# A DeltaNet and GELU-MLP kernel: the factors behind the GpSimd power, the bank of the second layer's last product, and the joins one block earlier

## The chip, the cores and the metric

The kernel runs on one core of one Trainium2 chip. The metric is device microseconds of one execution. Before the change the median of three runs is 658.57 us (658.12 to 659.23).

## The reference

Two parts, one after the other. The first is a DeltaNet layer over 4 x 8 sequences (batch x head) of 768 tokens with 48 channels each; the second is a two-layer MLP with exact GELU over the 3072 tokens, 384 -> 2048 -> 384. All is float32.

```python
k_n = k / (np.linalg.norm(k, axis=-1, keepdims=True) + 1e-06)
for t in range(S):                       # 768 steps, state (B, H, 48, 48)
    y[:, :, t] = einsum('bhd,bhde->bhe', q[:, :, t], state)
    v_old = einsum('bhde,bhd->bhe', state, k_n[:, :, t])
    state = state + beta_t * einsum('bhd,bhe->bhde', k_n[:, :, t], v_t - v_old)
x = y.transpose(0, 2, 1, 3).reshape(B * S, H * D)
h = x @ w_in
g = 0.5 * h * (1.0 + erf(h / sqrt(2)))
out = g @ w_out
```

## The kernel before, in words

**Tiling.** The 768 steps are cut into 12 chunks c of 64 tokens. A chunk has two units (a = 0, 1), each with two batches on the two halves of the 128 partitions and 8 heads. Within a chunk the recurrence becomes small matrix products: Gram products of the keys (`grams`), masked query-key products (`queries`, L459 puts the mask on them into P), a triangular system, and its solution. The system of two chunks, of four 32-row blocks a head, is handled at once: its 32 x 32 diagonal blocks are eliminated row by row (`eliminate`, L516 and L518, from chunk 4 on GpSimd), and the blocks below the diagonal are added by two *joins*, `join_both` (matmuls on L636): level 0 makes XM from G (results taken by VectorE on L648), level 1 makes Zf (L652). Around the elimination: `scales` (L486 and L491, needs the factors), `flip` (L496), `scaled_flip` (L501), then `back`: L527 turns Nu into XM, L531 into Zf, and L535 copies half of Zf on ScalarE.

**Factors.** The keys are not normalised; their factors gm are applied later. `norms` squares the keys on ScalarE, `prep` sums them on VectorE (L358) and takes the root as a power 0.5 on GpSimd (L360), and `finish` makes gm on VectorE (L307 to L311). `finish` waits for the power.

**The state.** For each chunk in turn: products with the state (psK, L710), subtraction (L721, L722, L727), `solve` (psU, L745; copied by ScalarE on L753 and L755), `use` and `update` (psY, L775 and L786), and `turns` (psX, L837), which transposes the outputs into xT for the MLP.

**The MLP.** From chunk 4 on it works on two chunks at once and uses a scheme with seven products for four blocks in both layers. The first layer runs in four blocks b; a block has eleven parts, in this order on TensorE (`part_of_layer`, matmuls on L977): P1 (X), P5 (Z), P6 (Y), P2 (X), R22 (Z), R11 (X), P7 (Y), P3 (V), R12 (V), P4 (Y), R21 (Y); the letters are PSUM tiles. P1, P5 and R22 are followed by copies on ScalarE; P6 by L1005 and L1036 on VectorE; P7 by L1013 (which reads Y and R22's copy, and before whose end P4 must not write Y) and a Gelu; R11 and R21 by Gelus; R12 by L1025. The second layer is seven products per chunk (matmuls on L911): 1 (X), 5 (Z), 2 (X), 6 (Y), 4 (X), 7 (Y), 3 (V). Its mixes of G are L1044, L1045 (mix 1), L1047 (mix 2) and L1049 (mix 3), its results are put together on L1079 to L1090; L1090 reads the last product, psV2.

**PSUM.** Eight banks: tag "dn" with two slots of two banks in rotation (psJ, psG, psK, psU, psY, psX of the DeltaNet part, and psV2), tag "mlp" with two slots, and one bank each for tags "z" and "sq"; psV of the first layer is in "sq".

**Order of the work.** Every step is put into a plan with a due time; one unit of time is one chunk. `emit` traces the steps by due time. VectorE's queue is exactly that order. The other engines' queues are set by a scheduler that starts from it; TensorE's MLP parts are chained, and `together` keeps steps of the DeltaNet part in one run on TensorE. Stage w (w = 4, 6, 8, 10) prepares chunks w and w+1 (elimination, joins, Gram products of w+2 and w+3, state) while the MLP of the chunks before runs. Due times of its steps are `begins`; n6, p6, n7, p7 are those of `norms` and `prep`; `turned_k` (L408) and `turned_q` (L413) transpose keys and queries on VectorE. Every engine takes its own queue in order, the DMA-issuing SP too.

Of the kernel before, what the change touches and what calls it, by code (L numbers as in the profile page):

```python
# [8 lines left out]
F32 = mybir.dt.float32  # L9
# [5 lines left out]
ALU = mybir.AluOpType  # L15
# [4 lines left out]
def kernel(  # L20
# [28 lines left out]
    nc = tc.nc  # L49
# [19 lines left out]
    small = [start.enter_context(tc.tile_pool(name="sq", bufs=2, space=bass.MemoryType.PSUM))]  # L69
    su = start.enter_context(tc.tile_pool(name="su", bufs=2))  # L70

    def dn(name):
        return ps.tile([128, 2, 512], F32, tag="dn", name=name)
# [225 lines left out]
    def heads(ap):  # L299
        return ap.rearrange("q (j r) d -> q r j d", r=2)  # L300
# [145 lines left out]
    def queries(us):  # L446
        c = us[0].c
        psP = products(us, 1)
        if c not in Ps:
            Ps[c] = (su if c == 1 else wk).tile([128, NA * H, C], F32, tag=f"P{c == 1}", name="P",  # L450
                                                bufs=1)
        for u in us:
            u.P = Ps[c][:, u.a * H:(u.a + 1) * H]
        dst = heads(Ps[c][:, us[0].a * H:(us[-1].a + 1) * H])
        if c < 2:
            nc.scalar.copy(dst, psP)
        else:
            both = mask.unsqueeze(1).to_broadcast([128, len(us) * H, C])
            nc.vector.tensor_tensor(dst, psP, heads(both), op=ALU.mult)  # L459

    def masked(u, engine=nc.gpsimd):
        engine.tensor_tensor(u.P, u.P, mask_h, op=ALU.mult)
# [163 lines left out]
    def join_both(g, level):  # L626

        xm, zf, off = XMs[g], Zf[g % 2], Gs[g]
        gm = gms[g].rearrange("q t h -> q (t h)")
        psJ = dn("psJ").rearrange("q b (k n) -> q b k n", n=2 * HB)  # L630
        for k in range(H):
            for cc in range(2):
                for p in range(2):
                    us = slice(2 * (cc * H + k), 2 * (cc * H + k) + 2)
                    rows = slice(p * C + level * HB, p * C + (level + 1) * HB)
                    nc.tensor.matmul(psJ[HALF[p ^ cc], p, k, :],  # L636
                                     lhsT=(xm if level else off)[rows, us, :],
                                     rhs=zf[rows, us, HB:C] if level else xm[rows, us, :],
                                     start=True, stop=True)
        for cc in range(2):  # L640
            for p in range(2):
                for e in range(2):
                    us = slice(2 * cc * H + e, 2 * (cc + 1) * H, 2)
                    at_ = (p ^ cc) * C + e * HB
                    src = psJ[at_:at_ + HB, p, :, e * HB:(e + 1) * HB]
                    if level == 0:
                        low_ = slice(p * C + HB, (p + 1) * C)
                        nc.vector.tensor_tensor(  # L648
                            xm[low_, us, :], src,
                            gm[low_, us].unsqueeze(2).to_broadcast([HB, H, HB]), op=ALU.mult)  # L650
                    else:
                        nc.vector.tensor_copy(zf[p * C:p * C + HB, us, HB:C], src)  # L652

    def gram_steps(c, part=(0,)):
        us = [tiles[c, a] for a in range(NA)]
# [193 lines left out]
    DH = DM // 2  # L849
# [50 lines left out]
    def of_g(c):  # L900
        g = Gp[c % 2 if c > 3 else 0]
        return [[g[:, a, k * FH:(k + 1) * FH] for k in range(2)] for a in range(NA)]

    W2 = {}
# [146 lines left out]
    def two(c, n):  # L1051
        A = of_g(c)
        if n == 1:
            W2["X"] = ps.tile([128, 2, DH], F32, tag="mlp", name="psX2")
            W2["o"] = [wk.tile([128, DM], F32, tag="o_sb", name="o_sb") for a in range(NA)]
            product(W2["X"][:, 0], A[0][0], B11, True)
        elif n == 5:
            W2["Z"] = small[0].tile([128, DH], F32, tag="z", name="psZ2")
            product(W2["Z"], W2["S"], T[1], True)
            W2["p1"] = more[0].tile([128, DH], F32, tag="p1", name="p1")  # L1060
            nc.scalar.copy(W2["p1"], W2["X"][:, 0])
        elif n == 6:
            W2["Y"] = ps.tile([128, 1, DH], F32, tag="mlp", name="psY2")
            product(W2["Y"][:, 0], A[0][0], T[2], True)
        elif n == 2:
            product(W2["X"][:, 0], A[0][1], B21, False)
        elif n == 7:
            product(W2["Y"][:, 0], A[1][0], T[3], False)
        elif n == 4:
            product(W2["X"][:, 1], A[1][1], T[4], True)  # L1070
        else:
            W2["V"] = dn("psV2")[:, 0, 0:DH]
            product(W2["V"], A[0][1], B22, True)

    def read2(c, n):
# [48 lines left out]
    def at(first, last, steps):  # L1124

        total, done, timed = sum(s[0] for s in steps), 0.0, []
        for w, *step in steps:
            timed.append((first + (last - first) * (done + 0.5 * w) / total, step))
            done += w
        return timed  # L1130
# [122 lines left out]
    def state_at(c, *times, first=(), second=()):  # L1253

        steps = state_steps(c, first, second)
        if len(times) > len(steps):
            steps = steps[:-1] + [(turn, tiles[c, a]) for a in range(NA)]
        return [(t, step) for t, step in zip(times, steps) if t is not None]

    plan = [at(c + 1 + 0.25 * (c == 1), c + 2 + 0.25 * (c == 0), ffn_steps(c)) for c in range(4)]  # L1260
# [31 lines left out]
    for c in range(3, NC):  # L1292
        t = c - (1.35 if c % 2 and c > 5 else 1.0)
        plan += [at(t, t + 0.01, [(1.0, load_v, c)])]
    for c in range(4, NC):
        us = [tiles[c, a] for a in range(NA)]
        even = c % 2 == 0
        for name, src, t in (("Kb", k, {4: 1.8, 5: 2.73, 6: 3.25, 7: 3.55}.get(c, c - (2.9 if even else 3.6))),
                             ("Qb", q, {4: 3.2, 5: 3.9}.get(c, c - (1.4 if even else 1.29)))):
            plan += [at(t, t + 0.01, [(1.0, load_blocks, c, name, src)])]  # L1300
        for name, t in (("Kn", {4: 2.1, 5: 2.74, 7: 4.24}.get(c, c - (2.1 if even else 2.84))),
                        ("Kp", {4: 3.6, 5: 4.3}.get(c, c - (0.6 if even else 0.85)))):
            plan += [at(t, t + 0.01, [(1.0, load_k, c, name)])]
        t = {4: 2.7262, 5: 2.955, 6: 3.5, 7: 4.31}.get(c, c - (2.7 if even else 2.98))
        plan += [at(t, t + 0.0005, [(1.0, turned_k, u) for u in us])]
        t = {4: 3.88, 5: 4.33}.get(c, c - (0.3 if even else 0.93))
        plan += [at(t, t + 0.01, [(1.0, turned_q, u) for u in us])]
    def gram(c):
        return [(grams, [tiles[c, a] for a in range(NA)])] if c < NC else []
# [1 line left out]
    def query(c):  # L1311
        return [(queries, [tiles[c, a] for a in range(NA)])]
# [18 lines left out]
    for c in (2, 3, *range(4, NC, 2)):  # L1331
        n = FH // blocks(c)
        for b in range(n):
            t = c + 1.06 + 0.2577 * b
            plan += [at(t, t + 0.001, [(1.0, add_p5)])]
        t = c + (1.42 if c < 4 else 1.93)
# [14 lines left out]
    for w in range(4, NC, 2):  # L1351
        more_to_come = w + 2 < NC
        if w == 4:
            begins = 0.21, 0.29, 0.36, 0.44, 0.52, 0.57, 0.63, 0.72, 0.82, 0.92
            n6, p6, n7, p7 = 0.2, 0.26, 0.43, 0.48
        else:
            begins = -0.21, -0.11, 0.0, 0.1, 0.21, 0.29, 0.38, 0.52, 0.67, 0.84
            n6, p6, n7, p7 = 0.15, 0.2, 0.38, 0.42
            t = -1.5 if w > 6 else -1.44
            plan += rows_of(w // 2, w, ((1, t, t + 0.001), (1, t + 0.02, t + 0.021), (1, t + 0.03, t + 0.031),  # L1360
                                        (31, t + 0.04, -0.6), (1, -0.29, -0.289), (1, -0.285, -0.284),
                                        (1, -0.283, -0.282)))
        begins = [w + t for t in begins]
        plan += [at(begins[0], begins[0] + 0.001, [(1.0, together, (join_both, w // 2, 0), *query(w))]),
                 at(begins[1], begins[1] + 0.001, [(1.0, together, (join_both, w // 2, 1), *gram(w + 2))]),
                 state_at(w, *begins[2:6], second=gram(w + 3)),
                 state_at(w + 1, *begins[6:], second=query(w + 1))]
        if more_to_come:
            plan += spread("gram", 2, begins[1] + 0.04) + spread("gram", 2, begins[1] + 0.06)
            plan += spread("gram", 4, begins[3] + 0.04)  # L1370
            plan += [at(w + n6, w + n6 + 0.001, [(1.0, norms, w + 2)]), at(w + p6, w + p6 + 0.001, [(1.0, prep, w + 2)]),
                     at(w + n7, w + n7 + 0.001, [(1.0, norms, w + 3)]), at(w + p7, w + p7 + 0.001, [(1.0, prep, w + 3)]),
                     at(w + p7 + 0.04, w + p7 + 0.041, [(1.0, finish, w + 2)])]
    with tc.manual_schedule(engines={mybir.EngineType.DVE}):
        emit(*plan)

# [29 lines left out]
```

## Time and profile before

| | us |
|---|---|
| median of the runs | 658.57 |
| the profiled execution | 658.88 |
| its span, first to last instruction | 656.3 |
| TensorE busy in the span | 616.1 |
| VectorE, ScalarE, GpSimd busy | 430.9, 247.7, 204.2 |
| stage 6: start of its MLP (280.2) to the start of the next (382.2) | 102.0 |
| stage 8: 382.2 to 484.4 | 102.2 |
| stage 10: 484.4 to 577.4 | 93.0 |
| MLP of chunks 10 and 11: 577.4 to 656.3 | 78.9 |

The stages hold the same MLP work; stages 6 and 8 have two runs of Gram products each that stage 10 lacks (64 matmuls in 1.09 us a run), and the last one has no DeltaNet work. A matmul's record begins when it starts and its modelled end can lie beyond the start of the next one, so the distance between the starts of two neighbouring parts is the time of the first: 0.87 us for a part of the first layer in stages 6 to 10, 2.6 for a product of the second, 1.09 for a run of 64 small matmuls.

### The profile page before, as it was taken

The page shows a single profiled execution, that of the slowest core. Times are in us where ns is not written, and L with a number is a line of the kernel's source. Part 1 is how long each engine was busy: PE and PEld are TensorE (multiplying, and loading weights), DVE is VectorE, ACT ScalarE, POOL GpSimd, SP SyncE. Part 2 cuts the span into 40 slices and gives each one's busy share as a digit, 9 for nine tenths or more (in the row PEclk, how much of TensorE's full clock was granted, in tenths as well). Part 3 has the DMA queues.
Part 4 walks back from the last instruction along what each step waited for, and adds up shares of the span by engine and source line. Part 5 has one row for each costly group of instructions (what it writes and reads, how often), then busy time and mean ns, then how long its engine had stood idle before and what let it go on. Part 6 is the DMA issues. An engine that isn't in the chain of part 4 may idle for free.

```text
span 656.3 us, 20825 instructions
## 1 busy us (share of the span) xinstructions
PE 616.1 (94%) x8998; PEld 550.1 (84%) x8998; DVE 430.9 (66%) x783; ACT 247.7 (38%) x552; POOL 204.2 (31%) x310
## 2 busy tenths in 40 slices
PE   5778999999999989899997999997999999999997
PEld 4666877766999988888797998797998789998997
DVE  6999989988757878445975554966542956332442
ACT  3576777424640453133632034442024422133300
POOL 4043002001588314882013884012686000000000
PEclk9568999999999989999998999999899999999999
DMA  9885673103443424231134321224120201010010
GB/s 134 173 264 156 130 188 109 25 2 63 70 70 54 86 36 69 54 65 21 17 55 70 73 53 23 25 41 72 38 49 1 25 3 25 3 25 1 0 25 24
DMA packets 158427, 39.69 MB, mean 60 GB/s; under 512 B 150016, under 2 KB 153216, under 8 KB 158336
## 3 DMA queue, kind: packets, MB, share of 16 engines
q1 hardware_dynamic: 155664, 37.34, 29.4%
q10 hardware_dynamic: 2672, 1.03, 0.8%
q8 instruction: 70, 1.15, 0.7%
q14 instruction: 21, 0.17, 0.1%
HBM read 33.62 MB, written 4.72 MB: 58 GB/s over the span
## 4 chain that ended last, share of the span: by engine, by line
PE 63%; DVE 20%; issue 8%; ACT 4%; DMA 2%; POOL 2%; SPq 1%; DVEq 0%; ACTq 0%; POOLq 0%
PE psX L911 10%; PE psY L977 9%; PE psX L977 7%; PE psY L911 6%; PE psZ L977 5%; PE psV L977 4%; PE psV L911 3%; DVE Nu L518 3%; DVE tmp L516 3%; PE psK L710 3%; PE psZ L911 3%; PE psO L878 2%; PE psH L860 2%; DVE XM L527 2%; PE psG L423 2%
## 5 line engine op out<-in xcount | busy, mean ns | idle before, releaser
L360 POOL TENSOR_TENSOR n<-n,half 128x16 f32<-128x16 f32 x10 | 30.0, 3003 | 218.8 <-DVE n L358 169.0
L518 POOL TENSOR_TENSOR Nu<-Nu,tmp 128x30 f32<-128x30 f32 (+14 forms) x120 | 65.1, 543 | 9.0
L516 POOL TENSOR_TENSOR tmp<-Nu 128x30 f32<-128x30 f32 (+14 forms) x120 | 61.9, 516 | 9.3
L977 PE MATMUL psX<-xT,w_in_sb 128*128 128x256 f32 (+1 forms) x288 | 62.8, 348 | 0.0
L911 PE MATMUL psX<-w_out_sb,G 128*128 128x192 f32 x320 | 60.3, 345 | 0.0
L911 PEld LDWEIGHTS psX<-w_out_sb,G 128*128 128x128 f32 x320 | 56.4, 202 | 0.8
L977 PEld LDWEIGHTS psX<-xT,w_in_sb 128*128 128x128 f32 x288 | 48.4, 193 | 5.1
L860 PE MATMUL psH<-xT,w_in_sb 128*128 128x256 f32 x192 | 44.3, 384 | 2.6 <-ACT G L960 2.0
L860 PEld LDWEIGHTS psH<-xT,w_in_sb 128*128 128x128 f32 x192 | 35.7, 190 | 9.8 <-ACT G L960 3.3
L878 PE MATMUL psO<-w_out_sb,G 128*128 128x384 f32 x128 | 43.9, 490 | 0.0
L1005 DVE TENSOR_TENSOR psY<-psY,pu 128x512 f32<-128x512 f32 x20 | 14.0, 698 | 43.3 <-PE psY L977 42.1
L977 PE MATMUL psY<-xT,w_in_sb 128*128 128x256 f32 (+1 forms) x192 | 41.6, 346 | 0.0
L960 ACT COPY xT<-psX 128x768 f32<-128x768 f32 x9 | 7.2, 800 | 89.8 <-PE psX L837 89.8
L960 ACT COPY pu<-psZ 128x512 f32<-128x512 f32 x40 | 23.5, 588 | 36.3 <-PE psZ L977 31.5
L878 PEld LDWEIGHTS psO<-w_out_sb,G 128*128 128x128 f32 x128 | 23.6, 190 | 14.0
L977 PEld LDWEIGHTS psY<-xT,w_in_sb 128*128 128x128 f32 x192 | 31.9, 191 | 3.3
L960 ACT ACTIVATE G<-G 128x512 f32<-128x512 f32 x40 | 25.2, 630 | 23.4 <-DVE G L1013 23.2
L1013 DVE TENSOR_TENSOR G<-psY,pu 128x512 f32<-128x512 f32 x20 | 13.8, 690 | 27.1 <-PE psY L977 26.9
L423 PE MATMUL psG<-Qt,Kt 48*64 48x64 f32 x768 | 18.0, 252 | 11.8 <-DVE o_sb L1090 7.7
L911 PE MATMUL psZ<-T,pu 128*128 128x192 f32 x160 | 28.3, 329 | 0.1
L911 PE MATMUL psY<-T,G 128*128 128x192 f32 x160 | 28.2, 329 | 0.0
L423 PEld LDWEIGHTS psG<-Qt,Kt 48*64 48x64 f32 x768 | 15.8, 163 | 14.6 <-DVE o_sb L1090 8.0
(197 smaller groups left out, 1384.2 us busy)
## 6 DMA issues: line engine op xcount, KB each, us to landing
Kp<-in_k_dram SPq DMA_DIRECT2D x76, 96.0 KB, 3.1
w_out_sb<-in_moe_w_in_dram SPq DMA_DIRECT2D x24, 256.0 KB, 4.2
w_raw<-in_moe_w_out_dram SPq DMA_DIRECT2D x16, 384.0 KB, 4.4
V<-in_v_dram SPq DMA_DIRECT2D x48, 96.0 KB, 3.1
out_dram<-o_sb SPq DMA_DIRECT2D x40, 96.0 KB, 2.2
Qp<-in_k_dram SPq DMA_DIRECT2D x64, 32.0 KB, 2.2
Qp<-in_q_dram SPq DMA_DIRECT2D x64, 32.0 KB, 2.1
Qp<-in_q_dram SPq DMA_DIRECT2D x16, 96.0 KB, 4.3
```

What stands on the lines that cost most here:

```text
L360: nc.gpsimd.tensor_tensor(flat, flat, half, op=ALU.pow)
L423: nc.tensor.matmul(psG[HALF[p], r, i * NP + j, :], lhsT=u.Kt[rows, p, j, :], rhs=(u.Qt if x else u.Kt)[rows, p, j, :], start=True, stop=True)
L516: rows_on.tensor_tensor(tmp, nu[:, j + 1:, j:j + 1].to_broadcast([128, n, j]), nu[:, j:j + 1, 0:j].to_broadcast([128, n, j]), op=ALU.mult)
L518: rows_on.tensor_tensor(nu[:, j + 1:, 0:j], nu[:, j + 1:, 0:j], tmp, op=ALU.add)
L710: nc.tensor.matmul(u.psK[to, x, r, j, :], lhsT=(u.Qt if x else u.Kt)[rows, p, j, :], rhs=St[rows, u.a, p ^ r, j, :], start=True, stop=True)
L860: nc.tensor.matmul(psH, lhsT=w_in_sb[:, f // 2, m, f % 2 * 128:(f % 2 + 1) * 128], rhs=xTs[c][:, m, :], start=(m == 0), stop=(m == NM - 1))
L878: nc.tensor.matmul(u.psO, lhsT=G[:, u.a, f, :], rhs=w_out_sb[:, f, :], start=(f == 0), stop=(f == NF - 1))
L911: nc.tensor.matmul(ps_, lhsT=lhs[:, f, :], rhs=rhs[:, f, :], start=first and f == 0, stop=f == FH - 1, skip_group_check=not first)
L960: i = fn(*args, **kw)
L977: nc.tensor.matmul(ps_[:, i], lhsT=lhs[:, f // 2, f % 2 * 128:(f % 2 + 1) * 128], rhs=rhs, start=first and i == 0, stop=True, skip_group_c ...
L1005: nc.vector.tensor_tensor(L1["Y1"], L1["Y1"], L1["pu"][:, 0], op=ALU.add)
L1013: nc.vector.tensor_tensor(half(1, 1), shaped(L1["Y1"]), shaped(L1["pu"][:, 0]), op=ALU.add)
```

## The change

Four things are edited.

1. psV2, the last product of the second layer, leaves the "dn" tag for the "sq" bank, which the first layer's psV uses.
2. The masking of the queries (L459) becomes a step of its own from chunk 4 on (`cover`), and the taking of a join's results (L648 or L652) becomes two steps (`take`), one per chunk of the pair. At level 0 the mask's step stands between the two halves.
3. In stages 6 to 10 the due times of both joins, of `back`, and of `against_state` of the first chunk move earlier, those of the elimination's start a little. L413 of even chunks moves earlier with them.
4. `prep` of the second chunk moves earlier and `finish` later, and L408 of chunk 7 and L413 of chunk 5 move later.

No instruction is added or removed on any engine. In VectorE's queue of stages 6 to 10 (L numbers of before): L413 twice, L1005, L1036, L527, L531, L1013, half of L648, L1025, L459, the other half of L648; later L1025 of the last block behind L721 and L727. In the second layer: L358 ahead of L1082, L1090 ahead of L307, and L1047 twice ahead of L459 and L496. On TensorE the first join and the query products stand between P7 and P3 of the third block (before: behind P1 of the fourth), the second join and the Gram products behind P6 of the fourth block (before: behind R22), and psK ahead of P3 (before: ahead of R21). On ScalarE L535 stands ahead of R22's copy of the third block (before: behind that block's P7 Gelu), and the squares of the second chunk ahead of L722. In stage 4 the second half of L648 follows L459, and L721 and L727 stand ahead of L408 and L413.

```diff
             both = mask.unsqueeze(1).to_broadcast([128, len(us) * H, C])
-            nc.vector.tensor_tensor(dst, psP, heads(both), op=ALU.mult)
+            masks[c] = lambda: nc.vector.tensor_tensor(dst, psP, heads(both), op=ALU.mult)
+            if c < 4:
+                masks[c]()
+
+    masks = {}
+
+    def cover(c):
+        masks[c]()
...
-        for cc in range(2):
+        def taken(cc):
             for p in range(2):
...
+        todo.append(taken)
+
+    todo = []
+
+    def take(cc):
+        todo[-1](cc)
...
-            W2["V"] = dn("psV2")[:, 0, 0:DH]
+            W2["V"] = small[0].tile([128, DH], F32, tag="sq", name="psV2")
             product(W2["V"], A[0][1], B22, True)
...
-        t = {4: 2.7262, 5: 2.955, 6: 3.5, 7: 4.31}.get(c, c - (2.7 if even else 2.98))
+        t = {4: 2.7262, 5: 2.955, 6: 3.5, 7: 4.38}.get(c, c - (2.7 if even else 2.98))
         plan += [at(t, t + 0.0005, [(1.0, turned_k, u) for u in us])]
-        t = {4: 3.88, 5: 4.33}.get(c, c - (0.3 if even else 0.93))
+        t = {4: 3.88, 5: 4.4}.get(c, c - (0.47 if even else 0.93))
         plan += [at(t, t + 0.01, [(1.0, turned_q, u) for u in us])]
...
         if w == 4:
             begins = 0.21, 0.29, 0.36, 0.44, 0.52, 0.57, 0.63, 0.72, 0.82, 0.92
-            n6, p6, n7, p7 = 0.2, 0.26, 0.43, 0.48
+            takes = 0.212, 0.214, 0.292, 0.294
+            n6, p6, n7, p7, f7 = 0.2, 0.26, 0.4, 0.44, 0.55
         else:
-            begins = -0.21, -0.11, 0.0, 0.1, 0.21, 0.29, 0.38, 0.52, 0.67, 0.84
-            n6, p6, n7, p7 = 0.15, 0.2, 0.38, 0.42
-            t = -1.5 if w > 6 else -1.44
+            begins = -0.33, -0.163, -0.06, 0.08, 0.21, 0.29, 0.38, 0.52, 0.67, 0.84
+            takes = -0.328, -0.255, -0.16, -0.158
+            n6, p6, n7, p7, f7 = 0.15, 0.2, 0.37, 0.41, 0.53
+            t = -1.46 if w > 6 else -1.44
             plan += rows_of(w // 2, w, ((1, t, t + 0.001), (1, t + 0.02, t + 0.021), (1, t + 0.03, t + 0.031),
-                                        (31, t + 0.04, -0.6), (1, -0.29, -0.289), (1, -0.285, -0.284),
-                                        (1, -0.283, -0.282)))
+                                        (31, t + 0.04, -0.6), (1, -0.42, -0.419), (1, -0.415, -0.414),
+                                        (1, -0.413, -0.412)))
         begins = [w + t for t in begins]
...
                  state_at(w + 1, *begins[6:], second=query(w + 1))]
+        plan += [at(w + t, w + t + 0.001, [(1.0, take, i % 2)]) for i, t in enumerate(takes)]
+        plan += [at(t, t + 0.001, [(1.0, cover, c)])
+                 for t, c in ((begins[0] + (0.004 if w == 4 else 0.07), w), (begins[7] + 0.03, w + 1))]
...
-                     at(w + p7 + 0.04, w + p7 + 0.041, [(1.0, finish, w + 2)])]
+                     at(w + f7, w + f7 + 0.001, [(1.0, finish, w + 2)])]
```

## The prediction

> **What bounds the kernel now.** I read the page's chain first, then TensorE's waits, then the timeline where the waits sit. All line numbers are those of the kernel before.
>
> ```profile
> PE 63%; DVE 20%; issue 8%; ACT 4%; DMA 2%; POOL 2%; SPq 1%; DVEq 0%; ACTq 0%; POOLq 0%
> ```
>
> Most of the chain is TensorE work, and from 280 us on nearly all of it. So a change pays there only if it removes TensorE idle time or half-clock time; both have to be found by place. The waits of TensorE (us in total, times, longest) name two that the change touches:
>
> ```profile
> PE psG L423 <- DVE o_sb L1090: 7.7, 2, 3.9
> ...
> PE psY L977 <- ACT G L960: 3.3, 3, 1.1
> ```
>
> The first falls in the second layer of stages 6 and 8 (a stage prepares chunks w and w+1; w = 4, 6, 8, 10). This is stage 6 (start, us, ..., [idle before <- releaser]):
>
> ```profile
> 352.08 1.15 PE L745 MATMUL psU<-V,Zf 64*64 64x48 f32 x64
> 357.10 1.98 PE L423 MATMUL psG<-Qt,Kt 48*64 48x64 f32 x64 [3.88 <-DVE o_sb L1090]
> 359.01 4.88 PE L911 MATMUL psX<-w_out_sb,G 128*128 128x192 f32 x16
> 363.73 2.76 PE L911 MATMUL psZ<-T,pu 128*128 128x192 f32 x16
> ...
> 354.80 0.18 DVE L307 TENSOR_SCALAR n<-n 128x32 f32<-128x32 f32 x1 [3.02 <-POOL n L360]
> ...
> 356.70 0.34 DVE L1090 TENSOR_TENSOR o_sb<-psV,o_sb 128x192 f32<-128x192 f32 x1
> ...
> 351.86 2.90 POOL L360 TENSOR_TENSOR n<-n,half 128x16 f32<-128x16 f32 x1 [12.56 <-DVE n L358]
> ```
>
> The query product psG needs the PSUM slot of the second layer's psV2, whose reader L1090 stands in VectorE's queue behind `finish` (L307 to L311), which waits 3.0 us for GpSimd's power (L360, 2.90 us). Meanwhile psX takes 4.88 us where its neighbour psZ, with as many matmuls, takes 2.76: the clock fell. The windows view shows when (stretch, its length, busy us of PE, PEld, DVE, ACT, POOL, then the granted clock):
>
> ```profile
> 233.44:236.85 3.41, 1.51 (x103) 1.39 (x95) 2.65 (x4) 0.49 (x1) 0.00 (x0) 1.00 0.15 21
> 236.85:240.27 3.42, 3.36 (x30) 3.26 (x30) 3.33 (x7) 1.35 (x3) 0.00 (x0) 0.50 0.29 35
> 264.15:267.57 3.42, 2.05 (x27) 1.84 (x18) 1.23 (x1) 1.28 (x5) 3.11 (x7) 1.00 0.29 55
> 352.90:356.32 3.42, 0.33 (x24) 0.20 (x16) 1.42 (x4) 1.89 (x6) 3.07 (x3) 1.00 0.26 44
> 356.32:359.73 3.41, 2.63 (x66) 2.51 (x67) 1.42 (x4) 0.00 (x0) 1.68 (x2) 0.50 0.27 61
> ```
>
> A stretch with TensorE busy 0.33 of 3.42 us is followed by half clock; so is one busy 1.51 of 3.41. One busy 2.05 of 3.42 is not.
>
> **Part 1: the bank, and `finish` moved behind L1090.** psV2 no longer rotates through the two-slot "dn" tag, so psG takes the slot of psK, whose readers (L721, L722) are done by 348 us. In the changed queue L358 stands ahead of L1082, and L1090 ahead of L307. Stage 10 has no `finish` and shows the undisturbed spacing: psU at 555.18, psZ at 559.91, 4.73 us. Stage 6 takes 352.08 to 363.73 = 11.65, stage 8 454.11 to 465.95 = 11.84. Gain 6.92 + 7.11 = **14.0 us** (per stage 3.9 idle, 0.9 of psG and 2.0 of psX at half clock). The new bank adds a wait of psV2 on L1025 (325 us, wanted at 349) and of the next layer's psV on L1090 (383.9, wanted at 388.2): nothing.
>
> What is late next: psY (L775) needs the mask L459, now its own step behind both L1047. In stage 6, on the old clock, psX would start at 354.3. The second L1047 ends some 3.6 us later, as in stage 10 (557.20; 560.11 + 0.69), at 357.9. L459 (1.23) ends at 359.1 and psY is due at 354.3 + 2.7 + 2.7 = 359.7. It fits by 0.6 us, if L307 to L311 (2.0 us), whose power now starts at about 349.4, end before 355.9; I cost it at nothing, and at 1 us per us that the power is late. The squares, moved up in ScalarE's queue, need the next chunk's keys: the four issues (2.7 us) start when the last squares end (335.7) and land 3.1 us later, 341.5, against 343.0. That cover is 1.5 us.
>
> **Part 2: the join moved into the third block.** Stage 6 before:
>
> ```profile
> 307.31 2.08 DVE L527 STREAM_TRANSPOSE XM<-Nu 128x1024 f32<-128x1024 f32 x1
> 309.27 1.95 DVE L531 STREAM_TRANSPOSE Zf<-Nu 128x1024 f32<-128x1024 f32 x1
> ...
> 309.62 1.16 PE L636 MATMUL psJ<-XM,G 32*64 32x64 f32 x64
> ...
> 311.25 2.10 ACT L535 COPY Zf<-Zf 32x1024 f32<-32x1024 f32 x2 [4.41 <-DVE Zf L531]
> ...
> 314.02 1.13 PE L977 MATMUL psY<-TX,Sw 128*128 128x256 f32 x4 [1.09 <-ACT G L960]
> ```
>
> The join costs about 1.3 us of idle here: 0.1 before L636, 1.1 at psY (its bank's Gelu stands behind L535 in ScalarE), 0.1 before the second join. Afterwards the first join and the query come after P7 of block 2, five products (4.3 us) earlier. In the changed queue of ScalarE, L535 stands *ahead* of R22's copy and R11's Gelu of that block, and VectorE does L531 ahead of L1013, which needs that copy. From the end of L527 (time 0): L531 1.95, L535 2.10, copy 0.6, L1013 0.7, hand-overs 0.1: L1013 ends at 5.4. TensorE joins at 0.2, then join and query 1.09 each, P3 0.97, R12 0.87: P4, which writes the bank that L1013 reads, is due at 4.25. **Idle 1.2 us.** Then half of L648 1.73, L1025 0.68, L459 1.23, the other half 1.73: XM is whole at 10.8, and the second join can start at 10.9. TensorE does P4, R21, P1, P5, P6 from 5.45 (4 x 0.87 + 0.97) and is due at 9.9. **Idle 1.0.** Behind that nothing is late: L652 (3.45) ends before psK is due.
>
> The first join itself waits for L527. Stage 6: L1036 ends at 303.5, GpSimd's rows at 298.5, L527 at 305.55; the slot is at 305.2 (P7 starts at 304.35): idle 0.6. Sum 2.8 against 1.3: **+1.4 us**.
>
> Stages 8 and 10: GpSimd now decides. Its elimination runs 38.6 us from L501 (362.36 to 400.96). In the changed stage 6, L496 follows L459 on a clock 1.4 us late: L501 at 359.1 + 1.9 + 0.1 + 1.4 = 362.5, hardly moved, while TensorE is 6.92 - 1.4 = 5.5 us ahead. The rows end at 401, L527 at 403, the join is at 403.2; its slot is at 406.38 + 0.87 - 5.5 = 401.7. Idle 1.5 + 1.2 + 1.0 = 3.7 against 1.3: **+2.4**. Stage 10 likewise (L501 4.5 us earlier than 464.39, rows end 498.5, join 500.8, slot 499.3): 3.7 + 0.15 against 1.9 (the page adds 0.6 before P4 there): **+1.9**. Stage 4: the second half of L648 now follows L459, so the second join waits 1.0 us, of which 0.3 is taken back where psK waits for L652 anyway: **+0.7**; the half-clock stretch after 236.85 may shift with it, worth up to 1.7 us less.
>
> **Other edits.** L413 earlier: Qt's data are long there (its loads end near 248 us for stage 6) and VectorE idles 3.7 us before L1005. On SP the key loads go ahead of the 16 query loads (8.7 us) and values stand among key blocks; the latest comer, the value rows for L385, lands near 354, and L385 stands before L491 and L501, which starts at 362: hidden by 4 us. On GpSimd two value products (0.83 us) move by up to two rows in stage 4. Instruction counts are the same on every engine. Nothing.
>
> **Sum.** -14.0 + 1.4 + 2.4 + 1.9 + 0.7 = -7.6 us. The profiled execution took 658.88 (span 656.3 and 2.6 around it), so 651.3; the median of the runs is 658.57, 0.3 lower: **651.0**.
>
> **A rule weighed.** The rows above show half clock after a TensorE idle of 1.96 us. The Trainium skill (TensorE: Matmul & The Clock Gate, "Why this matters for your kernels") warns only of idle gaps over about 3 us, because it wants one whole idle window. By it my 1.5 us waits never cost clock and the sum stays 651.0; by the rows they could, and a second rival has that price.
>
> **Rivals.**
> (a) The join's waits do not appear, as intended: then only the 14.0 is left, 644.5, and with the old 1.3 + 1.3 + 1.9 gone as well 640. For it: ScalarE and VectorE idle much in these blocks. Against: the order in their queues. 0.12.
> (b) One or two clock drops, or the mask late after a late power. A drop costs 2.9 us as at 356 (0.9 + 2.0). Stage 8's first join leaves TensorE busy 1.9 of 3.4 us if the wait falls in one stretch, between the 1.51 that dropped and the 2.05 that did not. 653.9 to 656.8. 0.22.
> (c) Slower: the clock drops at the joins of all three stages for two stretches each, 3 x 3.4 = 10.2, 661. It decides from a busy share under some 0.5 in each stage; stage 6, with 0.6 and 1.2 idle four us apart, speaks against. 0.08.
> (d) The drops take back the gain almost exactly, within 0.2%: 0.05.
>
> **Numbers.** Main case 0.53, at 648 to 654. A measurement tells 0.2% (1.3 us) from no change. Range 646.5 to 656.5: all of the main case, half of (a), nearly all of (b), about 0.8. Faster 0.53 + 0.12 + 0.22 = 0.87, same 0.05, slower 0.08.
>
> **What would show it.** Right: no wait of psG on L1090; full clock after 350 and 453 us; L1090 ahead of L307. Right for the joins: P4's psY waiting on L1013 by 1.2 us in three stages, L1013 waiting on ScalarE's copy behind L535; the second join waiting on L648; the first join in stages 8 and 10 waiting on L527, and L527 on GpSimd's L518. Wrong: psY (L775) waiting on L459, half clock beside a join, or no wait at P4.

## The result and the profile after

The changed kernel takes 648.82 us (median of 4 runs, 647.99 to 649.38) against 658.35 for the kernel before (4 runs, 658.05 to 659.23): ratio 0.985, 95% interval 0.9835 to 0.9869. That is 9.5 us less; 7.6 less, 651.0, was predicted. The profiled execution took 647.99, its span 646.3.

Kernels made from the changed one have its line numbers: L527, L531, L535 are now L534, L538, L542; L496 and L501 are L503 and L508; L518 is L525; L648 and L652 are L655 and L659; L1013, L1025, L1036 are L1027, L1039, L1050; L1047 is L1061; L1090 is L1104; L775 is L789; the matmul lines L636, L710, L745, L911 and L977 are L643, L724, L759, L925 and L991, and ScalarE's L960 is L974.

The second layer of stage 6 first (the timeline of the changed kernel; columns as before):

```profile
353.60 1.15 PE L759 MATMUL psU<-V,Zf 64*64 64x48 f32 x64
353.70 0.36 DVE L1104 TENSOR_TENSOR o_sb<-psV,o_sb 128x192 f32<-128x192 f32 x1 [1.32 <-PE psV L925]
353.98 0.17 DVE L307 TENSOR_SCALAR n<-n 128x32 f32<-128x32 f32 x1
354.56 1.13 PE L423 MATMUL psG<-Qt,Kt 48*64 48x64 f32 x64
355.62 2.87 PE L925 MATMUL psX<-w_out_sb,G 128*128 128x192 f32 x16
358.32 2.76 PE L925 MATMUL psZ<-T,pu 128*128 128x192 f32 x16
```

psU to psZ is 4.72 us (11.65 before). L1104 stands ahead of L307, psG starts when psU's matmuls are through, and psX takes 2.87 instead of 4.88: there is no half-clock stretch here any more. What TensorE now waits for from 280 us on (its waits; us in total, times, longest):

```profile
PE psY L991 <- DVE G L1027: 3.4, 3, 1.1
PE psJ L643 <- DVE XM L655: 1.6, 3, 0.5
PE psJ L643 <- DVE XM L534: 1.4, 3, 0.6
```

All three belong to the moved joins. The timeline of stage 6's third block shows the first two:

```profile
303.76 2.10 DVE L534 STREAM_TRANSPOSE XM<-Nu 128x1024 f32<-128x1024 f32 x1
305.92 1.16 PE L643 MATMUL psJ<-XM,G 32*64 32x64 f32 x64 [0.22 <-DVE XM L534]
307.75 2.10 ACT L542 COPY Zf<-Zf 32x1024 f32<-32x1024 f32 x2 [5.22 <-DVE Zf L538]
309.88 0.59 ACT L974 COPY pu<-psZ 128x512 f32<-128x512 f32 x1
310.49 0.69 DVE L1027 TENSOR_TENSOR G<-psY,pu 128x512 f32<-128x512 f32 x1 [2.78 <-ACT pu L974]
...
311.24 1.13 PE L991 MATMUL psY<-TX,w_in_sb 128*128 128x256 f32 x4 [1.15 <-DVE G L1027]
...
316.62 1.14 PE L643 MATMUL psJ<-Zf,XM 32*64 32x64 f32 x58 [0.53 <-DVE XM L655]
```

Read it backwards from P4 at 311.24: it waits for L1027, that for R22's copy at 309.88, and the copy for L542 ahead of it in ScalarE's queue, although R22's product was long done: its matmuls ended at 304.0, and ScalarE had idled 5.22 us until L538. In stage 8 the first join waits longer, and its L534 is now released by GpSimd:

```profile
400.46 2.08 DVE L534 STREAM_TRANSPOSE XM<-Nu 128x1024 f32<-128x1024 f32 x1 [0.32 <-POOL Nu L525]
...
402.60 1.16 PE L643 MATMUL psJ<-XM,G 32*64 32x64 f32 x64 [0.61 <-DVE XM L534]
```

On the page GpSimd's share of the chain grew from 2% to 11% accordingly:

```profile
PE 59%; DVE 21%; POOL 11%; issue 4%; DMA 2%; ACT 2%; SPq 0%; DVEq 0%; POOLq 0%
```

The stage lengths (start of a stage's MLP to the start of the next, from the profiled executions) tell the kernels apart more sharply than the medians do. The start of stage 6 itself lay between 278.3 and 282.2 us over 14 profiles, without any order that follows the edits, so what lies before it is left out. "rest" is stage 11 to the end of the span; "issue" is a TensorE wait in stage 8 for nothing that the profile shows, which some profiles have and others of the same kernel have not.

| kernel | stage 6 | stage 8 | stage 10 | rest | issue in stage 8 |
|---|---|---|---|---|---|
| before | 102.0 | 102.2 | 93.0 | 78.8 | |
| changed | 96.3 | 96.7 | 93.7 | 79.1 | |
| changed, second profile (after_again) | 96.3 | 96.9 | 93.7 | 79.0 | |
| bank | 95.1 | 95.1 | 93.0 | 78.8 | |
| finish | 95.1 | 95.3 | 93.0 | 78.8 | |
| bank_finish | 95.1 | 95.4 | 93.0 | 78.9 | |
| joins | 102.0 | 104.9 | 93.6 | 78.8 | 1.0 |
| prep_early | 96.7 | 96.7 | 93.1 | 78.9 | |
| after_copy_late | 94.0 | 94.6 | 91.5 | 79.0 | |
| copy_late_again | 94.0 | 95.8 | 91.5 | 78.8 | 1.0 |
| after_whole | 95.4 | 97.8 | 92.8 | 78.8 | 1.5 |
| after_flip | 97.9 | 98.9 | 93.3 | 79.0 | 0.6 |
| bank_copy_late | 94.6 | 95.4 | 92.8 | 78.8 | 1.3 |
| mask_first | 94.0 | 95.2 | 91.0 | 78.8 | 0.8 |

### The profile page after: what moved, and what is told of

Its sections match the earlier page's. It is cut to its first block, busy times and chain, and to the rows that moved or that the text cites. A ratio compares the mean times of both kernels' runs of the same rounds, so it can differ in the third digit from the quotient of the medians.

```text
span 646.3 us, 20824 instructions
## 1 busy us (share of the span) xinstructions
PE 614.1 (95%) x8998; PEld 547.5 (85%) x8998; DVE 428.8 (66%) x783; ACT 248.5 (38%) x552; POOL 203.3 (31%) x310
## 3 DMA queue, kind: packets, MB, share of 16 engines
HBM read 33.62 MB, written 4.72 MB: 59 GB/s over the span
## 4 chain that ended last, share of the span: by engine, by line
PE 59%; DVE 21%; POOL 11%; issue 4%; DMA 2%; ACT 2%; SPq 0%; DVEq 0%; POOLq 0%
PE psX L925 10%; PE psY L925 7%; PE psY L991 6%; POOL Nu L525 5%; PE psX L991 5%; POOL tmp L523 5%; PE psV L991 4%; PE psK L724 3%; PE psZ L991 3%; PE psV L925 3%; DVE Nu L525 3%; DVE tmp L523 3%; PE psZ L925 3%; PE psO L892 3%; PE psG L423 2%
## 5 line engine op out<-in xcount | busy, mean ns | idle before, releaser
L360 POOL TENSOR_TENSOR n<-n,half 128x16 f32<-128x16 f32 x10 | 30.0, 3002 | 209.6 <-DVE n L358 159.8
L525 POOL TENSOR_TENSOR Nu<-Nu,tmp 128x30 f32<-128x30 f32 (+14 forms) x120 | 65.2, 544 | 9.1
L991 PE MATMUL psX<-xT,w_in_sb 128*128 128x256 f32 (+1 forms) x288 | 63.0, 349 | 0.0
L925 PE MATMUL psX<-w_out_sb,G 128*128 128x192 f32 x320 | 56.1, 329 | 0.0
L991 PEld LDWEIGHTS psX<-xT,w_in_sb 128*128 128x128 f32 x288 | 48.7, 194 | 5.1
L925 PEld LDWEIGHTS psX<-w_out_sb,G 128*128 128x128 f32 x320 | 52.2, 190 | 0.7
L974 ACT COPY xT<-psX 128x768 f32<-128x768 f32 x9 | 7.2, 800 | 91.3 <-PE psX L851 91.3
L991 PE MATMUL psY<-xT,w_in_sb 128*128 128x256 f32 (+1 forms) x192 | 41.3, 344 | 0.0
L974 ACT COPY pu<-psZ 128x512 f32<-128x512 f32 x40 | 23.5, 587 | 34.7 <-PE psZ L991 34.6
L991 PEld LDWEIGHTS psY<-xT,w_in_sb 128*128 128x128 f32 x192 | 32.1, 191 | 3.3
L1027 DVE TENSOR_TENSOR G<-psY,pu 128x512 f32<-128x512 f32 x20 | 13.8, 690 | 31.1 <-PE psY L991 22.6
L974 ACT ACTIVATE G<-G 128x512 f32<-128x512 f32 x40 | 25.3, 632 | 15.5 <-DVE G L1027 15.2
L925 PE MATMUL psZ<-T,pu 128*128 128x192 f32 x160 | 28.3, 329 | 0.1
L925 PE MATMUL psY<-T,G 128*128 128x192 f32 x160 | 28.2, 329 | 0.0
L925 PE MATMUL psY<-w_out_sb,G 128*128 128x192 f32 x160 | 28.0, 328 | 0.0
L925 PE MATMUL psX<-T,G 128*128 128x192 f32 x160 | 27.7, 327 | 0.0
```

Source lines behind the costliest of these rows:

```text
L360: nc.gpsimd.tensor_tensor(flat, flat, half, op=ALU.pow)
L525: rows_on.tensor_tensor(nu[:, j + 1:, 0:j], nu[:, j + 1:, 0:j], tmp, op=ALU.add)
L925: nc.tensor.matmul(ps_, lhsT=lhs[:, f, :], rhs=rhs[:, f, :], start=first and f == 0, stop=f == FH - 1, skip_group_check=not first)
L974: i = fn(*args, **kw)
L991: nc.tensor.matmul(ps_[:, i], lhsT=lhs[:, f // 2, f % 2 * 128:(f % 2 + 1) * 128], rhs=rhs, start=first and i == 0, stop=True, skip_group_c ...
L1027: nc.vector.tensor_tensor(half(1, 1), shaped(L1["Y1"]), shaped(L1["pu"][:, 0]), op=ALU.add)
```

## The experiments

The theory: bank and late `finish` remove the 14.0 us stall, the joins give back some 3.5 us. The main rival: a part of the gain is the joins'. The first four kernels take the change apart.

### bank: psV2 alone

```diff
-            W2["V"] = dn("psV2")[:, 0, 0:DH]
+            W2["V"] = small[0].tile([128, DH], F32, tag="sq", name="psV2")
```

> The kernel before with one edit: psV2 takes the sq bank. The queues are those of the kernel before; finish still stands ahead of L1090 in VectorE. Theory (the stall is the wait of psG for the PSUM slot that L1090 frees late; L1090 itself is wanted by nobody soon): the whole 14.0 us goes with the bank alone, ratio 0.979, about 644.4; psU to psZ 4.7 in stages 6 and 8, and L1090 still some 3 us late. Rival 1 (the order of VectorE's queue is what counts, since the mask L459 stands behind finish as well): a part of the stall comes back as a wait of psY on L459, gain 7 to 10 us. Rival 2 (the gain of the changed kernel comes from the joins): no gain.

Measured: 644.67 us, ratio 0.980 (0.977 to 0.9835). Stages 6 and 8 are 6.9 and 7.1 us shorter, stage 10 is as before. The timeline of its stage 6:

```profile
353.62 1.15 PE L745 MATMUL psU<-V,Zf 64*64 64x48 f32 x64
354.58 1.13 PE L423 MATMUL psG<-Qt,Kt 48*64 48x64 f32 x64
...
358.24 0.34 DVE L1090 TENSOR_TENSOR o_sb<-psV,o_sb 128x192 f32<-128x192 f32 x1
```

L1090 is as late as ever (4.6 us behind psV2's end, behind `finish`), and TensorE no longer waits for it: the stall was the wait for the slot. No wait on L459 appears, so rival 1 is out, and with the joins in their old place rival 2 is out too.

### finish: the queue order alone

(in stage 4 likewise, with f7 = 0.55)

```diff
-            n6, p6, n7, p7 = 0.15, 0.2, 0.38, 0.42
-            t = -1.5 if w > 6 else -1.44
+            n6, p6, n7, p7, f7 = 0.15, 0.2, 0.38, 0.42, 0.53
+            t = -1.46 if w > 6 else -1.44
...
-                     at(w + p7 + 0.04, w + p7 + 0.041, [(1.0, finish, w + 2)])]
+                     at(w + f7, w + f7 + 0.001, [(1.0, finish, w + 2)])]
```

> The kernel before with finish (L307 to L311) due behind L1090 in stages 4, 6 and 8, and the elimination's start a little later as that requires; psV2 stays in the dn rotation. Theory: psV2 ends as psU starts, L1090 takes 0.34 us and ends before psU's 64 matmuls do (1.0 us), so psG finds its slot free: the whole 14.0 us, about 644.4; either of the two edits is enough. Rival (the bank is needed, the order alone isn't enough, because L358 and L1082 to L1087 still stand ahead of L1090): psG keeps waiting 1 to 2 us twice, gain 10 to 12 us if the clock stays at 1.00, 4 to 8 if it drops.

Measured: 645.49 us, ratio 0.982 (0.979 to 0.986); stages 6 and 8 as short as with the bank. From 280 us on the trace has no wait of psG on L1090. Either edit is enough: the rival that the bank is needed is out.

### bank_finish: both, without the joins

The edits of the two kernels above, with n7 and p7 as in the changed kernel:

```diff
-            n6, p6, n7, p7 = 0.15, 0.2, 0.38, 0.42
+            n6, p6, n7, p7, f7 = 0.15, 0.2, 0.37, 0.41, 0.53
```

> The changed kernel without its joins: bank, finish behind L1090, squares and power earlier; the joins, the takes and the masks where the kernel before has them. Theory (the two edits overlap, and the joins cost what their spans show: P7 of the third block to the second layer's first product got longer by 1.2, 1.6 and 0.7 us, and stage 4 by 0.3): 644.4 to 645.2, 3.6 to 4.5 us faster than the changed kernel. Rival (the earlier joins are needed once TensorE is 7 us ahead, because GpSimd's elimination or the masks would be late otherwise): 648 or more.

Measured: 646.74 us, ratio 0.983 (0.980 to 0.986). The runs of these three kernels spread by 3.6 to 4.6 us, so their medians don't rank them; the stage lengths do: 95.1, 95.4, 93.0, the same as either edit alone, so the two overlap fully. Stages 6, 8 and 10 are 1.2, 1.3 and 0.6 us shorter than in the changed kernel, 3.1 in all; 3.6 to 4.5 was expected.

### joins: the joins alone

```diff
-            W2["V"] = small[0].tile([128, DH], F32, tag="sq", name="psV2")
+            W2["V"] = dn("psV2")[:, 0, 0:DH]
...
-            n6, p6, n7, p7, f7 = 0.15, 0.2, 0.37, 0.41, 0.53
+            n6, p6, n7, p7, f7 = 0.15, 0.2, 0.38, 0.42, 0.46
```

(made from the changed kernel, in stage 4 likewise)

> The changed kernel without bank and finish: psV2 in the dn rotation, norms, prep and finish due as in the kernel before; the joins one block earlier, taken in halves. Theory: the stall of psG stays (14.0 us), and the joins cost 1.2 in stages 6 and 8 (GpSimd is not late there, since TensorE isn't ahead), 0.7 in stage 10 and 0.3 in stage 4: slower than the kernel before by about 3.4 us, 661.8. Rival (the joins give a part of the gain): faster than the kernel before by 1 us or more.

Measured: 659.95 us against 657.54, ratio 1.0036 (1.0013 to 1.0058), 2.4 us slower. The psG wait is there twice with 3.9 us. Stage 6 is no longer than before because psU to psZ took 10.4 instead of 11.65 us here (stage 8: 11.5 instead of 11.8): in stage 6 half clock lasted one stretch of 3.4 us, not two (stretch, its length, busy us of PE, PEld, DVE, ACT, POOL, then the granted clock):

```profile
353.21:356.62 3.41, 0.23 (x13) 0.23 (x17) 2.26 (x6) 1.29 (x5) 2.55 (x4) 1.00 0.15 23
356.62:360.04 3.42, 3.42 (x70) 3.30 (x63) 0.00 (x0) 0.00 (x0) 1.18 (x1) 0.50 0.38 76
```

The rival that the joins give part of the gain is out.

### after_copy_late: L542 out of the way

The joins are made to be hidden, so what breaks the cover? Here only the third step of `back` is due later, behind the first half of L655 in the plan; in ScalarE's queue L542 then stands behind R11's Gelu and the Gelu of P7.

```diff
-                                        (1, -0.413, -0.412)))
+                                        (1, -0.3, -0.3+0.001)))
```

> The changed kernel with one step of back due 0.11 to 0.12 later: in ScalarE's queue its L542 (the copy of half of Zf, 2.10 us) no longer stands ahead of R22's copy but behind R11's Gelu and the Gelu of P7. The other queues are the same. Compared by the profiled runs from the start of stage 6's MLP to the end of the span (changed kernel 365.8 us; what lies before differs by up to 2 us from run to run in unchanged work). Theory (P4 waits for L1027, L1027 for the copy, the copy stands behind L542; what follows in VectorE's queue hangs on L1027 too): the wait of P4 goes (3 x 1.15) and the second join's wait on L655 with it (3 x 0.5), 5.0 us less, 360.8. Rival 1 (VectorE is late by itself: L538 and half of L655 are the bound): P4's wait shrinks to 0.3 to 0.7 and the second join keeps its 0.5, 1.5 to 2.5 us less. Rival 2 (L542 in its new place holds up R21's Gelu and with it P6's bank): the 1.1 us wait comes back at P6, no gain.

Measured: 642.58 us, ratio 0.979 (0.976 to 0.983); 359.1 from stage 6's start to the end. Stage 6 of its trace:

```profile
308.81 0.67 DVE L1027 TENSOR_TENSOR G<-psY,pu 128x512 f32<-128x512 f32 x1
309.00 1.04 ACT L542 COPY Zf<-Zf 32x1024 f32<-32x1024 f32 x1 [2.27 <-DVE Zf L538]
...
310.30 1.03 PE L991 MATMUL psV<-xT,w_in_sb 128*128 128x256 f32 x4
311.17 1.03 PE L991 MATMUL psY<-TX,w_in_sb 128*128 128x256 f32 x4
```

L1027 runs before L542 and ends 1.7 us ahead of P4, which follows R12 with the usual 0.87. The wait on L655 is gone too. The gain, 2.1 to 2.3 us a stage, is above the idle times of the records (1.15 + 0.53), because a wait's record starts at the modelled end of the matmul before: by the starts, P4 was 1.31 late (309.06 + 0.87 = 309.93, it started at 311.24) and the second join 0.77 (six of its matmuls, some 0.1 us, ran from 315.75, the others from 316.62). So what the joins cost came from one copy's place in a queue: nothing else was moved in the queues of TensorE, VectorE, ScalarE and GpSimd.

### after_whole: no halves

```diff
-            takes = -0.328, -0.255, -0.16, -0.158
+            takes = -0.328, -0.327, -0.16, -0.158
```

> The changed kernel with both halves of the first join's results taken at once, ahead of L1039 and the mask L459 in VectorE's queue. Theory (the second join waits for the second half, which stands behind 0.7 + 1.2 us of other work): the wait on L655 goes, 3 x 0.5 = 1.5 us less, 364.3 from stage 6's start to the end against 365.8; L1039 and L459 end 1.7 us later, which nobody waits for. Rival (the halves are there because the mask frees the PSUM slot that the Gram products behind the second join take): these wait for L459 instead, no gain or a loss up to 1 us.

Measured: 646.72 us, ratio 0.985 (0.981 to 0.988), which the runs don't tell from the changed kernel. In the trace the wait on L655 is gone in all three stages, no wait on L459 came in its place, and stages 6 and 10 are 0.9 us shorter; stage 8 is 1.1 us longer with an "issue" wait of 1.46 in it, 0.4 shorter without. The theory holds: with L542 ahead, taking the results in halves cost 0.4 to 0.9 us a stage.

### after_flip: an earlier elimination

```diff
-            plan += rows_of(w // 2, w, ((1, t, t + 0.001), (1, t + 0.02, t + 0.021), (1, t + 0.03, t + 0.031),
+            plan += rows_of(w // 2, w, ((1, t, t + 0.001), (1, t + 0.0051, t + 0.0052), (1, t + 0.03, t + 0.031),
```

> The changed kernel with flip (L503) due ahead of both L1061 in VectorE's queue in stages 6 and 8, so that GpSimd's elimination for stages 8 and 10 can start some 4 us earlier (its L508 waited 4.83 us for L503 in stage 8). Theory (GpSimd decides the first join of stages 8 and 10): their wait on L534 falls from 0.6 to 0.2, as in stage 6, and the elimination's rows end 3 to 4 us earlier; 0.8 us less, 365.0. P4's wait stays. Rival 1 (VectorE decides, L534 stands behind L1050): rows end earlier, but the join waits as before, 365.8. Rival 2 (L503 delays L1061 and the mask, psY L789 waits): a loss of 0.5 to 1 us per stage, 367.

Measured: 650.94 us, ratio 0.992 (0.989 to 0.995): slower than the changed kernel. What the theory said of the first joins and the loss of rival 2 both came: the first joins of stages 8 and 10 wait 0.22 and 0.19 instead of 0.61 and 0.59, but the mask is late, in stages 6 and 8 alike (stage 6):

```profile
357.03 3.42 DVE L1061 TENSOR_TENSOR G<-pu,G 128x512 f32<-128x512 f32 x2
357.27 2.64 POOL L508 TENSOR_TENSOR Nu<-Nu,XM 128x1024 f32<-128x1024 f32 x1 [0.66 <-DVE Nu L503]
360.37 1.21 DVE L459 TENSOR_TENSOR P<-psG,mask 128x1024 f32<-128x1024 f32 x1
361.73 0.68 PE L789 MATMUL psY<-V,P 64*64 64x48 f32 x32 [1.57 <-DVE P L459]
```

Stages 6 and 8 lose 1.6 us each. L503 alone didn't do it. The two L1061 took 0.66 and 2.84 us, the second from 357.6, just behind the start of GpSimd's L508, to 360.45, 0.5 us behind its end at 359.91; in the changed kernel the pair takes 0.84 and 0.69. With 0.69 for the second as well the mask would have ended at 359.4, ahead of psY, which was due at 360.1.

### bank_copy_late: the copy late, the joins in their old place

```diff
-                                        (1, -0.283, -0.282)))
+                                        (1, -0.2, -0.2+0.001)))
```

(on top of bank)

> The kernel before with the bank edit and L535 due later, so that in ScalarE's queue it stands behind R21's Gelu (first half) and P1's copy (second half). Theory (P6... that is, psY behind the first join, waits 1.08 us in three stages for R21's Gelu, which stands behind L535): these three waits go, 3.2 us less than with the bank alone: 358.9 from stage 6's start to the end against 362.1, and about 641 in all, faster than the kernel before and the changed one. Rival (L535 is then late for the second join's results L652, and psK or solve wait for Zf): the 1 us comes back as a wait on Zf, no gain.

Measured: 644.87 us, ratio 0.982 (0.9785 to 0.986). The expectation was mostly wrong: the three waits of 1.08 are gone, but stages 6 and 10 gain only 0.4 and 0.3 us, and stage 8, less its "issue" wait, 0.9. In stage 6:

```profile
317.79 3.44 DVE L652 COPY Zf<-psJ 32x256 f32<-32x256 f32 x8
321.26 0.69 DVE L1013 TENSOR_TENSOR G<-psY,pu 128x512 f32<-128x512 f32 x1
...
322.01 1.13 PE L977 MATMUL psY<-TX,w_in_sb 128*128 128x256 f32 x4 [0.56 <-DVE G L1013]
```

The rival had the right sign and the wrong place: it is not Zf that is late but L1013 of the last block, queued in VectorE behind the 3.44 us of L652. With the joins moved (after_copy_late), L652's counterpart L659 is over 1.0 us before the L1027 that corresponds to that L1013 starts, and no such wait appears. So the earlier join and the later copy need each other: the copy alone brings 0.3 to 0.9 us a stage, the earlier join alone costs 0.6 to 1.6, both together bring 1.1, 0.5 and 1.6 us in stages 6, 8 and 10 (0.2 in stage 8 in copy_late_again, less its "issue" wait).

### after_again, copy_late_again and mask_first

The changed kernel, the version with the late copy, and that version with another order in VectorE's queue of the second layer: L459, L503, L1061, L1061, so that L1061 is the one that meets L508.

```diff
-            plan += rows_of(w // 2, w, ((1, t, t + 0.001), (1, t + 0.02, t + 0.021), (1, t + 0.03, t + 0.031),
+            plan += rows_of(w // 2, w, ((1, t, t + 0.001), (1, t + 0.0051, t + 0.0052), (1, t + 0.03, t + 0.031),
...
-                 for t, c in ((begins[0] + (0.004 if w == 4 else 0.07), w), (begins[7] + 0.03, w + 1))]
+                 for t, c in ((begins[0] + (0.004 if w == 4 else 0.07), w), (begins[7] + (0.03 if w == 4 else 0.0212), w + 1))]
```

> The changed kernel as it is, beside the next two kernels on the same chip. Every theory: about 648.8, 365.8 us from stage 6's start to the end of the span, 0.985 of the kernel before.

> The changed kernel with L542 later in ScalarE's queue, as measured once before (359.0 us from stage 6's start to the end of the span), now beside the changed kernel. Theory (the two waits behind L542 cost the joins their gain): 6.5 us under the changed kernel on the same chip. Rival (the difference came in part from another chip): 5 or less.

> As the last one, and in VectorE's queue of the second layer the mask L459 and L503 ahead of both L1061 (in stage 10 the mask alone), instead of L1061, L459, L503. Theory (L1061 ran 2.85 us beside GpSimd's L508 against 0.69 alone, and that, not its place, made the mask late when L503 was put first): the mask ends before psX does, the elimination starts 3 us earlier, L1061 is slowed but needed only 4 us later; the first joins of stages 8 and 10 wait 0.2 instead of 0.8 and 0.6, 1.0 us less than copy_late_again, 358.0 from stage 6's start to the end. Rival (L1061 late holds up the state update L805 and the next product psY of the second layer): a loss of 1 us or more.

Measured side by side on one chip (kernel before 657.83), in this order: 649.12, ratio 0.988 (0.985 to 0.990); 641.78, ratio 0.976 (0.973 to 0.979); 641.30, ratio 0.976 (0.973 to 0.978). The late copy is 7.3 us under the changed kernel by the medians, 5.7 by the spans from stage 6's start, and 6.7 without the "issue" wait of 1.0; 6.5 was expected, and 5 or less by the rival. mask_first does what was expected by its profile, though its median can't be told from its neighbour's: the first joins of stages 8 and 10 wait 0.23 and 0.20, the span from stage 6's start is 1.1 us shorter, as expected (359.1 against 360.2, with an "issue" wait of 0.8 and 1.0 in it), and L1061 is slowed to 3.41 us for the pair with TensorE not waiting for the mask:

```profile
355.51 1.18 DVE L459 TENSOR_TENSOR P<-psG,mask 128x1024 f32<-128x1024 f32 x1
358.50 3.41 DVE L1061 TENSOR_TENSOR G<-pu,G 128x512 f32<-128x512 f32 x2
```

That settles what made the mask late in after_flip. The version with the late copy and mask_first beat both the kernel before and the changed one. From 280 us on TensorE's waits in mask_first sum to 1.4 us.

### prep_early: the price of a shorter stall

```diff
-            n6, p6, n7, p7 = 0.15, 0.2, 0.38, 0.42
+            n6, p6, n7, p7 = 0.15, 0.2, 0.37, 0.41
```

> The kernel before with the squares and the power of the second chunk earlier in stages 6 and 8 (as in the changed kernel), bank and place of finish as before: the power L360 starts 2.0 to 2.5 us earlier, so that the wait of psG on L1090 shrinks from 3.9 to 1.4 to 1.9 us. Theory 1 (what costs clock is the TensorE idle time in one 3.4 us stretch, and 1.96 us was enough at 235 us): the clock still falls behind it in at least one of the two stages, gain 4 to 6 us, 652.5 to 654.5. Theory 2 (a wait under 2 us costs no clock, as the waits of the changed kernel's joins did not): gain 2 x (2.0 to 2.5) + 2 x 2.9 = 9.8 to 10.8, 647.7 to 648.7.

Measured: 647.50 us, ratio 0.985 (0.982 to 0.988). Theory 2 gave the number. psG waits 1.41 us twice, psU to psZ is 6.35 and 6.36, and the clock stays full. The power L360 starts 2.5 us earlier, counted from the stage's start. That alone, with the slot and the place of `finish` as they were, brings 10.8 of the 14.0 us. The stretch with the wait, then one at 233 us of the same profile and the one behind it (columns as before):

```profile
352.88:356.29 3.41, 2.00 (x110) 1.68 (x111) 2.26 (x6) 1.87 (x6) 2.55 (x4) 1.00 0.41 77
...
233.42:236.83 3.41, 1.46 (x96) 1.33 (x88) 3.01 (x5) 0.10 (x1) 0.00 (x0) 1.00 0.20 28
236.83:240.24 3.41, 3.41 (x26) 3.35 (x18) 2.85 (x6) 1.43 (x3) 0.00 (x0) 0.50 0.28 34
```

The first, busy 2.00 of 3.41, costs no clock; the second, busy 1.46, does.

## Why the prediction was right

**Part 1 was right to the tenth.** Predicted 6.92 + 7.11; the bank alone takes 6.94 and 7.11 out of stages 6 and 8. The mask was predicted to end 0.6 us ahead of psY: L459 ended at 360.35 and psY started at 361.02, without a wait. The nothing costed for the new bank's two waits, for L413, for the DMA queues and for L385 was right: from 280 us on TensorE waits for none of them. What the prediction didn't see is that the two edits do the same thing: either alone gives all of it.

**Part 2 had the mechanisms right and the sizes of two terms too large.** The edit of Part 2 is what is left when the bank alone is taken from the changed kernel, so its terms are measured as changed less bank:

| term | predicted | measured |
|---|---|---|
| stage 6 | +1.4 | +1.2 |
| stage 8 | +2.4 | +1.6 |
| stage 10 | +1.9 | +0.6 |

- Stage 6: its parts 0.6, 1.2 and 1.0 add up to 2.8, which is 1.5 above 1.3, not the 1.4 that was entered. The first join was 0.38 late by the starts, not 0.6.
- "P4 idle 1.2": 1.31 by the starts, in the predicted chain (L535 ahead of R22's copy, L1013 behind that).
- "Second join idle 1.0": 0.77. XM was whole at 316.5, but six matmuls that need only the first half had run already, which the step left out.
- "The first join of stages 8 and 10 idles 1.5": 0.77 and 0.74 by the starts, with the cause as predicted (L527 on L518, so GpSimd decides). The rows took 38.1 us from L501, not 38.6 (L501 itself 2.36 instead of 2.63), and L527 ended at 402.5 instead of 403, while TensorE reached the slot at 401.83 instead of 401.7. The difference of two late times has the errors of both; this one was twice too large.
- Stage 10: the three waits sum to 2.8 by the starts, not to 3.85; with +0.6 measured, the kernel before lost 2.2 there by the difference, not 1.9.

**Stage 4** (+0.7) can't be settled: stage 6 starts 0.3 later than before in the first profile and 0.04 earlier in the second, inside the spread.

**The sum.** The profiled executions differ by 10.9: 5.7 in stage 6, 5.5 in stage 8, less 0.6 in stage 10, 0.3 before stage 6 and 0.3 in the rest, and 0.9 outside the span (1.7 against 2.6 around it), which nothing in the edit explains. By the medians it is 9.5, 1.9 more than forecast; the mis-sized joins, 0.2 + 0.8 + 1.3 = 2.3, cover that.

**The rivals.** (a) "the joins' waits do not appear" is out: they do, and with two of the three taken away by the late copy the time lies where (a) had it (640 to 644.5): 642.6 and 641.8. (b) and (c) are out: no stretch beside a join of stages 6 to 10 fell to half clock in any of the kernels, and in these stages psY waited for the mask only in after_flip, where it was pushed.

**The rule weighed.** The rows won over the rule, but what they measure is not the length of one wait. In these profiles half clock comes in fixed stretches of 3.41 us, and it goes with the time that TensorE was busy in the stretch before. Between 200 and 630 us, in all 14 profiles, every stretch at full clock with TensorE busy 1.78 us or less was followed by half clock, and none busy 2.00 us or more was. In between both happened: 1.85, 1.90 and 1.96 were followed by it, 1.83, 1.84, 1.90 and 1.95 were not. Ahead of 200 us this is no guide: stretches busy 2.29 (after_again, 39 us) and 2.35 (after_flip, 41 us) were followed by half clock, and one busy 1.74 (after_copy_late, 62 us) was not. The same 1.97 us wait of psK in stage 4 cost a stretch in the changed kernel, where it lay inside one (busy 1.45), and none in mask_first, where two shared it (busy 2.64 and 2.00). The stretches with the moved joins kept 2.26 us or more busy in the changed kernel, so by these rows their waits, 1.2 us at the longest, had to cost no clock. The Trainium skill (TensorE: Matmul & The Clock Gate, "Why this matters for your kernels") warns of gaps over about 3 us only; here 1.97 us were enough when they fell into one stretch.

## What to carry to other kernels

When the waits name an engine's instruction as the releaser, look at what stands ahead of it in that engine's queue: here the stall could be cured at the slot, at the queue, or nearly at the power that the queue waited for, and the three don't add up. When work is moved into a gap, follow every engine that serves it, ScalarE's copies too: a 2.1 us copy that nobody needed for another 8 us (until L659 overwrites its source) turned a gain of the joins into a loss, and once it was moved the joins paid. Price a wait that is the difference of two late times by bounds, and measure stage by stage where the whole run spreads more than the effect.

## What the runs showed of the hardware

- **A VectorE operation can stand still for a GpSimd one.** L1061 (two inputs in SBUF, 128x512) takes 0.65 to 0.69 us. Started 0.34 us after GpSimd's L508 it took 2.84 and ended 0.5 us behind it; in bank and mask_first as well (the pair 3.40 and 3.41). It ended as far behind in the kernel before, where it started late in L501's time (1.61 us), and in finish beside L491 (1.74 us). The L1061 that had started 0.2 us before L508 took its usual 0.66. The Trainium skill (SBUF — State Buffer, "SBUF: two separate sides") calls the port pair of the two an exclusive lock that blocks the other for the whole instruction; the traces agree. So the order of VectorE's queue also decides what the hit costs: with the mask behind the slowed L1061 TensorE lost 1.57 us, with the mask ahead of it nothing.
- **Full clock takes a busy stretch to come back.** Stretches at half clock that were busy 2.63 and 3.00 us of 3.41 (the kernel before, 356 and 459 us) were followed by another at half; one busy 3.42 (joins, 357 us) by full clock. Between 200 and 630 us of all profiles those busy 2.24 to 3.00 us stayed at half, those busy 3.29 or more did not. That is the difference between 11.65 and 10.4 us for the same stall.
- **"issue" waits come and go.** The same stage 8 had none in one profile of the late copy and 0.95 us in another; what causes them stays open.
